# Loads cut into other pieces, a planner with other landing times, and raw products in the last two column pieces of a fused FFT-filter and GeGLU kernel

## The chip, the cores and the metric

The kernel runs on one core of one Trainium2 chip. The metric is the device time of one execution in microseconds (us). The core's engines are named as the profile names them: PE (matrix multiply, with its weight loads as PEld), DVE (vector), ACT (activation functions and copies), POOL (GpSimd) and SP, which here does nothing but issue DMAs.

## The reference

One input x (2048 x 640, bf16) is layer-normalised row by row into xn. Two branches start from xn and meet at the end:

```
xn = layernorm(x)
s  = irfft2(rfft2(xn) * (w_r + 1j * w_i))              # a filter in the frequency plane
g  = silu((gelu(xn @ w_gate) * (xn @ w_up)) @ w_down)  # 640 -> 1536 -> 640
out = x + s * g
```

## The kernel before, in words

**Tiles.** The 2048 rows are sixteen slabs of 128 rows (n1 = 0 to 15), kept in `X`. The hidden size 1536 is cut into twelve tiles of 128 (t), the slabs into four groups of four (grp).

**The GeGLU branch.** `gate_up(grp, t)` (L878) makes two psum tiles: five matmuls of 512 columns into `pg` (gate) and five into `pu` (up), all at L891. ACT turns `pg` into `ge` with Gelu (L904), DVE multiplies `pu` by `ge` into `uT` (L908). There are two buffers each of `pg` and `pu` and three of `ge`, so the gate matmuls of tile t+2 wait for the Gelu of tile t, and the up matmuls of t+2 for the product of t. `down(n1)` (L935) then makes one slab's 640 output columns from twelve `uT` tiles and `Wd` (L969), in two pieces of 320 columns, 2 x 6 matmuls each; the last slab (n1 = 15) has three pieces of 256, 256 and 128 columns. A piece goes through a tanh on ACT (L978) and a product on DVE (L983), which together are SiLU; `finish` (L951, L956) multiplies by the filter branch y and adds x.

**The start.** The first four slabs are transposed on PE while they are still raw (`turn_raw`, L461) and copied into `XR` (L297; helper `copy_on`, as are all copies out of psum). The first two hidden tiles of group 0 run on these raw rows (L891 with `XR`); their results wait in `IU` and `R` and are normalised later on DVE (L921, L923) with the rows' means and deviations. For this those 2 x 4 x 128 numbers are turned on PE (L570), copied (L572, tile `th`), stored to DRAM (`D5`) and loaded back as a broadcast to all partitions (`RB`, 512 KB). Column sums of the first weights come from one-column matmuls (L472). From slab 4 on, normalised slabs are transposed by DMA (L502).

**The filter branch.** `fold` adds and subtracts mirrored halves on DVE (L511 to L525), a DFT of 128 points follows on PE (L538, L539), ACT copies the result into `mc` (two buffers), and a DMA stores it to DRAM (`D2`, one store for each pair of slabs, eight in all). When all eight are stored, DRAM is read back regrouped (`BU`, L583), and `spectral` (L659 to L778) and `inverse` (L812 to L836) do the rest of the transform.

**The order.** Nothing in the program's order is left to the hardware. Every piece of work is a `Task` with an engine, a cost, a rank and its predecessors; `Plan.run` plays them through with the costs written in the code, always taking the ready task of best rank, and the engines' instruction streams are emitted in the order that it finds. `Plan.ready` gives the time from which a task may start: the latest of its predecessors' ends plus `MARGIN` (250 ns for PE, 60 ns for the others). A DMA's end is `land` where one is given; otherwise it is the modelled end on the wire (340 bytes per ns) plus a term that depends on when it was issued. So a changed cost does not change what an engine does, but when the plan lets it do it: the order on all engines may change.

**The loads.** All loads of the start but one are issued by SP, in the order in which the code adds them: 0.4 to 1 us of SP for one, so that the order on SP is the order on the wire. A DMA that SP issues also waits until the DMA eight places before it on the hardware queues has landed, since completions go round eight semaphores.

Of the kernel before, what the change touches and what calls it, by code (L numbers as in the profile page):

```python
# [13 lines left out]
ACT = mybir.ActivationFunctionType  # L14
ALU = mybir.AluOpType
P = 128
S = 2048
D = 640
# [96 lines left out]
class Plan:  # L115
# [21 lines left out]
    def ready(self, t, e, now):  # L137
        for a in t.after:
            if a.done is None:
                return None  # L140
        for a in t.order:
            if a.start is None:
                return None
        at = max([0.0] + [a.start + a.engs[e][0] if a.on == e == "PE" else a.done + (0 if a.on == e and not a.size else self.MARGIN[e] + ((1500 if a.size else 250) if e == "PE" and a.start > 20000 else 0)) for a in t.after])
        more = {}
        for s in t.new:
            mine = self.slots[s.tag]
            k = len(mine) - self.bufs[s.tag] + more.get(s.tag, 0)
            more[s.tag] = more.get(s.tag, 0) + 1
            if k >= 0:  # L150
                for u in mine[k].users:
                    if u.done is None:
                        return None
                    at = max(at, u.done + self.MARGIN[e])
        if t.size and e == "SP":
            at = max(at, self.wire - self.BACKLOG)
        return at

    def run(self):
        left, now, order = list(self.tasks), 0.0, []  # L160
        while left:
            best, soon, held = None, None, {}
            for t in left:
                if t.hold:
                    for e in t.engs:
                        at = self.ready(t, e, now)
                        if at is not None and now < at <= now + t.hold:
                            held[e] = min(held.get(e, t.rank), t.rank)
            for t in left:
                for e in t.engs:  # L170
                    at = self.ready(t, e, now)
                    if at is None:
                        continue
                    at = max(at, self.free[e])
                    if at <= now and e in held and held[e] < t.rank:
                        at = now + 20
                    if at <= now and len(t.engs) > 1 and e == "DVE" and max(now, self.free["ACT"]) + t.engs["ACT"][0] <= now + t.engs[e][0] + self.PREFER:
                        at = max(now, self.free["ACT"]) + 20
                    if at <= now:
                        if best is None or (t.rank, t.seq) < (best[0].rank, best[0].seq):  # L180
                            best = (t, e)
                    elif soon is None or at < soon:
                        soon = at
            if best is None:
                if soon is None:
                    raise AssertionError("the plan is stuck at %d of %d" % (len(order), len(self.tasks)))
                now = soon
                continue
            t, e = best
            occ, lat = t.engs[e]  # L190
            t.on, t.start = e, now
            self.free[e] = now + occ
            if VERB: print(f"{now:9.0f} {occ:6.0f} {t.done or 0:9.0f} {e} {t.emit.__qualname__.split('kernel.<locals>.')[-1]} {t.rank}")
            t.done = now + lat
            if t.land:
                self.wire = max(self.wire, t.land - 3200)
                t.done = t.land
            elif t.size:
                self.wire = max(self.wire, now + occ + 900) + t.size * t.slow / 340.0
                t.done = self.wire + (1000 if now < 1000 else 2100 if now < 1700 else 2600 if now < 2700 else 3300 if now < 18000 else 2600 if now < 21000 else 1000) + t.lag  # L200
            for s in t.new:
                self.slots[s.tag].append(s)
            order.append(t)
            left.remove(t)
        return order
# [17 lines left out]
def kernel(  # L223
# [11 lines left out]
    nc = tc.nc  # L235
# [95 lines left out]
    def load_w(sb, view, got, a, b, land=0):  # L331
        cs = slice(a * P, b * P)
        seq[0] += 1
        w = dma(sb[:, :, cs], view[:, :, cs], (0, -4, seq[0]), (b - a) * 163840, slow=1.1, land=land)
        for t in range(a, b):
            got[t] = w
# [33 lines left out]
                                 start=True, stop=True, skip_group_check=True)  # L370
        return add(go, "PE", (n * ns, n * ns), rank, after=after, new=[] if heat.users else [heat], use=[idle] + ([heat] if heat.users else []))
    seq[0] += 1
    x_in[0] = add(lambda e: None, "SP", (1, 1), (0, -5), size=1, land=3550)
    load_w(Wg, gv, g_in, 0, 2, land=4500)
    load_x(1, 2, land=4950)
    load_w(Wu, uv, u_in, 0, 2, land=6150)
    load_x(2, 3, land=6600)
    load_x(3, 4, land=7100)
    t = add(blank, "DVE", (330, 400), (0, -9), new=[idle])
    t = warmed = keep_warm(6, [t])  # L380
    load_gu(2, 4)
# [1 line left out]
    load_tab("f1")  # L383
    load_x(6, 8)
    load_gu(4, 6)
    load_x(8, 10)
    load_gu(6, 8)
    load_x(10, 12)
    load_gu(8, 10)
    load_x(12, 16)  # L390
    load_gu(10, 12)
    load_d(0, 8)
    load_d(8, 12)


    aps, roots = {}, {}
# [538 lines left out]
    def down(n1):  # L935
# [26 lines left out]
        for lo, hi, tag in parts:  # L962
            ps, th, mm = Slot(tag), Slot("th"), []
            for k in range(0, 12, 6):
                def go(e, k=k, lo=lo, hi=hi, ps=ps):
                    if k == 0:
                        place(ps, (512,))
                    for i in range(k, k + 6):
                        nc.tensor.matmul(ps.tile[:, 0:hi - lo], lhsT=uT[grp, ks[i]].tile[:, j * P:(j + 1) * P], rhs=Wd[:, ks[i], lo:hi],  # L969
                                         start=(i == 0), stop=(i == 11))  # L970
                step[0] += 1
                mm.append(add(go, "PE", c_pe(*[hi - lo] * 6), (1, step[0]), new=[] if k else [ps],
                              after=[u_done[grp, t] for t in ks[k:k + 6]] + mm + [d_in[t] for t in ks[k:k + 6]],
                              use=[uT[grp, t] for t in ks[k:k + 6]] + ([ps] if k else [])))

            def tanh(e, lo=lo, hi=hi, ps=ps, th=th):
                place(th, (320,), FP32)
                nc.scalar.activation(out=th.tile[:, 0:hi - lo], in_=ps.tile[:, 0:hi - lo], func=ACT.Tanh, scale=0.5)  # L978

            def silu(e, lo=lo, hi=hi, ps=ps, th=th):  # L980
                if lo == 0:
                    place(G2, (D,))
                nc.vector.scalar_tensor_tensor(out=G2.tile[:, lo:hi], in0=th.tile[:, 0:hi - lo], scalar=1.0, in1=ps.tile[:, 0:hi - lo],  # L983
                                               op0=ALU.add, op1=ALU.mult)
            def early(e, lo=lo, hi=hi, ps=ps):
                place(yp, (hi - lo,), FP32)
                nc.vector.tensor_tensor(out=yp.tile, in0=y.tile[:, n1 % 2, lo:hi], in1=ps.tile[:, 0:hi - lo], op=ALU.mult)

            def late(e, lo=lo, hi=hi, th=th):
                nc.vector.scalar_tensor_tensor(out=yg.tile[:, lo:hi], in0=th.tile[:, 0:hi - lo], scalar=1.0, in1=yp.tile,  # L990
                                               op0=ALU.add, op1=ALU.mult)
            a = add(tanh, "ACT", c_act(hi - lo), (0, step[0]), after=mm[-1:], new=[th], use=[ps])
            if last and hi == D:
                yp = Slot("mc")
                t = add(early, "DVE", c_dve(hi - lo, 1, True), (0, step[0]), after=mm[-1:] + [y_done[n1]], new=[yp], use=[ps, y])
                t = add(late, "DVE", c_dve(hi - lo, 1), (0, step[0]), after=[a, t] + done, use=[th, yp, yg])
                t = add(lambda e, lo=lo: nc.vector.tensor_tensor(out=res.tile[:, lo:], in0=yg.tile[:, lo:], in1=sx.tile[:, lo:], op=ALU.add),
                        "DVE", c_dve(hi - lo), (0, step[0]), after=[t, xr], use=[yg, sx, res])
                add(lambda e, lo=lo: nc.scalar.dma_start(out=outv[:, n1, lo:], in_=res.tile[:, lo:]), "ACT", (430, 430), (0, 0, n1),
                    after=[t], use=[res], size=256 * (hi - lo))  # L1000
                continue
            done.append(add(silu, "DVE", c_dve(hi - lo, 1, True), (0, step[0]), after=[a] + done, new=[] if lo else [G2],
                            use=[ps, th, G2] if lo else [ps, th]))
            if last:
                finish(lo, hi, [done[-1]], (0, step[0]), lo == 0)
# [42 lines left out]
```

## Time and profile before

| | |
|---|---|
| median of 4 runs | 204.67 us (204.38 to 204.81) |
| the profiled execution's own time | 204.43 us |
| its span in the trace | 202.7 us, so 1.7 us lie around it |
| granted TensorE clock | 0.999 |
| PE busy | 196.0 us, 97% of the span |
| DVE, ACT, POOL busy | 146.8, 127.3, 33.7 us |
| DMA in the first 30 us | 320 to 395 GB/s from slice 2 to slice 6 of 40, mean 161 GB/s over the span |
| last matmul ends, last store issued, span ends | 198.3, 200.06, 202.7 us |

A matmul of N columns counts as busy longer than it holds the engine, because matmuls overlap: five of 512 columns appear as a row of 1.24 us but the next group starts 1.08 us after them (0.216 us each). A stall on PE is therefore read from the distance of starts, not only from the idle column. Six matmuls of 320 columns take 0.81 us in this sense, twelve 1.63 us, and one 128-column matmul at the start 0.056 us.

### The profile page before, as it was taken

The page shows a single profiled execution, that of the slowest core. Times are in us where ns is not written, and L with a number is a line of the kernel's source. Part 1 is how long each engine was busy: PE and PEld are TensorE (multiplying, and loading weights), DVE is VectorE, ACT ScalarE, POOL GpSimd, SP SyncE. Part 2 cuts the span into 40 slices and gives each one's busy share as a digit, 9 for nine tenths or more (in the row PEclk, how much of TensorE's full clock was granted, in tenths as well). Part 3 has the DMA queues.
Part 4 walks back from the last instruction along what each step waited for, and adds up shares of the span by engine and source line. Part 5 has one row for each costly group of instructions (what it writes and reads, how often), then busy time and mean ns, then how long its engine had stood idle before and what let it go on. Part 6 is the DMA issues. An engine that isn't in the chain of part 4 may idle for free.

```text
span 202.7 us, 4151 instructions
## 1 busy us (share of the span) xinstructions
PE 196.0 (97%) x1547; PEld 117.8 (58%) x1547; DVE 146.8 (72%) x314; ACT 127.3 (63%) x228; POOL 33.7 (17%) x72
## 2 busy tenths in 40 slices
PE   7999999999999999999999999999999999999991
PEld 2994443567544554677755554567755555557781
DVE  3689849999522227999999989963326987778782
ACT  4998759984543466687776757433276666765521
POOL 2413134599400000000000000000000222112212
PEclk9999999999999999999999999999999999999999
DMA  6999999568883958664430411014900333344422
GB/s 174 325 320 338 335 395 218 127 84 203 215 287 113 375 161 243 115 144 138 128 114 24 129 65 65 3 65 129 418 38 0 108 83 108 102 127 129 132 100 65
DMA packets 35398, 32.62 MB, mean 161 GB/s; under 512 B 10798, under 2 KB 32306, under 8 KB 35378
## 3 DMA queue, kind: packets, MB, share of 16 engines
q1 hardware_dynamic: 33938, 29.49, 49.0%
q0 software_dynamic: 1152, 2.66, 5.7%
q10 hardware_dynamic: 288, 0.20, 0.6%
q8 instruction: 12, 0.20, 0.4%
q14 instruction: 8, 0.07, 0.1%
HBM read 22.51 MB, written 9.19 MB: 156 GB/s over the span
## 4 chain that ended last, share of the span: by engine, by line
PE 79%; DMA 10%; DVE 6%; SPq 2%; issue 1%; ACT 1%; DVEq 0%; ACTq 0%
PE pg L891 20%; PE pu L891 20%; PE pg L969 11%; PE pu L969 11%; DMA RB<-D 4%; DMA D<-th 3%; PE sp L703 3%; PE sp L836 3%; PE sp L778 2%; PE sp L812 2%; DMA X<-in_A_x_dram 2%; PE sp L676 2%; SPq L502 1%; DMA D<-in_A_w_r_dram 1%; PE sp L696 1%
## 5 line engine op out<-in xcount | busy, mean ns | idle before, releaser
L891 PE MATMUL pg<-xnT,Wg 128*128 128x512 bf16 (+1 forms) x245 | 57.3, 366 | 0.3 <-ACT ge L904 0.3
L891 PE MATMUL pu<-xnT,Wu 128*128 128x512 bf16 (+1 forms) x245 | 57.3, 366 | 0.0
L908 DVE TENSOR_TENSOR uT<-pu,ge 128x512 bf16<-128x512 f32 x46 | 31.7, 688 | 27.5 <-PE pu L891 25.2
L904 ACT ACTIVATE ge<-pg 128x512 bf16<-128x512 f32 x46 | 27.3, 596 | 30.6 <-PE pg L891 30.5
L969 PEld LDWEIGHTS <-uT 128*128 128x128 bf16 x396 | 37.7, 98 | 14.3 <-issue 0.4
L891 PEld LDWEIGHTS <-Wg 128*128 128x128 bf16 x285 | 25.2, 98 | 23.9 <-issue 0.6
L891 PEld LDWEIGHTS <-Wu 128*128 128x128 bf16 x285 | 24.8, 98 | 20.7 <-issue 0.3
L932 POOL DMA_DIRECT2D xr<-in_A_x_dram x16 | 8.8, 550 | 133.0 <-DVE res L956 133.0
L969 PE MATMUL pg<-Wd,uT 128*128 128x320 bf16 (+2 forms) x204 | 30.5, 293 | 0.0
L969 PE MATMUL pu<-Wd,uT 128*128 128x320 bf16 (+1 forms) x192 | 29.5, 297 | 0.1
L297 ACT CAST ma<-sp 128x644 bf16<-128x644 f32 (+1 forms) x32 | 23.4, 794 | 7.4 <-PE sp L703 3.4
L297 ACT CAST IU<-sp 128x640 bf16<-128x640 f32 x16 | 10.7, 693 | 3.9 <-PE sp L778 3.9
L297 ACT CAST Vt<-sp 128x640 bf16<-128x640 f32 x16 | 10.8, 691 | 3.7 <-PE sp L812 3.7
L978 ACT ACTIVATE th<-pg 128x320 f32<-128x320 f32 (+2 forms) x17 | 7.2, 426 | 9.3 <-PE pg L969 8.6
L297 ACT CAST mc<-sp 128x640 bf16<-128x640 f32 x16 | 10.6, 699 | 4.0 <-DMA D<-mc 3.9
L983 DVE SCALAR_TENSOR_TENSOR G<-th,pg 128x320 bf16<-128x320 f32 (+1 forms) x16 | 7.7, 478 | 6.2 <-ACT th L978 6.1
L978 ACT ACTIVATE th<-pu 128x320 f32<-128x320 f32 (+1 forms) x16 | 7.0, 439 | 8.0 <-PE pu L969 7.9
L983 DVE SCALAR_TENSOR_TENSOR G<-th,pu 128x320 bf16<-128x320 f32 (+1 forms) x16 | 7.7, 479 | 5.6 <-ACT th L978 5.5
L431 POOL TENSOR_TENSOR RSTD<-MVA,mh 128x1 f32<-128x1 f32 x12 | 8.9, 746 | 2.9 <-DVE MVA L413 2.2
L416 ACT ACTIVATE th<-X 128x640 bf16<-128x640 bf16 x11 | 8.1, 737 | 0.5 <-DMA D<-th 0.4
L756 DVE TENSOR_TENSOR R<-Y 64x644 bf16<-64x644 bf16 x16 | 7.8, 490 | 0.4
L758 DVE TENSOR_TENSOR R<-Y 64x644 bf16<-64x644 bf16 x16 | 7.8, 486 | 0.3
(110 smaller groups left out, 240.1 us busy)
## 6 DMA issues: line engine op xcount, KB each, us to landing
BU<-D SPq DMA_DIRECT2D x8, 640.0 KB
D<-mc SPq DMA_DIRECT2D x8, 320.0 KB
xr<-in_A_x_dram POOLq DMA_DIRECT2D x16, 160.0 KB, 3.5
D<-IU SPq DMA_DIRECT2D x8, 320.0 KB
out_dram<-res SPq DMA_DIRECT2D x15, 160.0 KB
Wg<-in_B_w_gate_dram SPq DMA_DIRECT2D x6, 320.0 KB
Wu<-in_B_w_up_dram SPq DMA_DIRECT2D x6, 320.0 KB
WF<-D SPq DMA_DIRECT2D x8, 161.0 KB
```

The lines of the kernel that those rows point to most:

```text
L297: return nc.scalar.copy(out=out, in_=in_) if e == "ACT" else nc.vector.tensor_copy(out=out, in_=in_)
L416: nc.scalar.activation(out=place(junk, (D,)), in_=x, func=ACT.Copy, scale=-1.0 / D, accum_out=less)
L431: nc.gpsimd.tensor_tensor(out=rstd, in0=var, in1=mh, op=ALU.pow)
L756: nc.vector.tensor_tensor(out=o, in0=Yf[:, ::-3, :], in1=Yf[:, 1:3, :], op=ALU.subtract)
L758: nc.vector.tensor_tensor(out=o, in0=Y[:, 0], in1=Y[:, 1], op=ALU.add)
L891: nc.tensor.matmul(ps.tile[:, lo:hi], lhsT=w[:, c, t * P:(t + 1) * P], rhs=XR[:, c, lo:hi] if early else xnT[:, c, grp * 512 + lo:grp * 51 ...
L904: nc.scalar.activation(out=ge.tile, in_=pg.tile if src is None else src, func=ACT.Gelu_apprx_tanh)
L908: nc.vector.tensor_tensor(out=u.tile, in0=pu.tile if src is None else src, in1=ge.tile, op=ALU.mult)
L932: nc.gpsimd.dma_start(out=sx.tile, in_=xv[:, n1, :])
L969: nc.tensor.matmul(ps.tile[:, 0:hi - lo], lhsT=uT[grp, ks[i]].tile[:, j * P:(j + 1) * P], rhs=Wd[:, ks[i], lo:hi], start=(i == 0), stop=(i ...
L978: nc.scalar.activation(out=th.tile[:, 0:hi - lo], in_=ps.tile[:, 0:hi - lo], func=ACT.Tanh, scale=0.5)
L983: nc.vector.scalar_tensor_tensor(out=G2.tile[:, lo:hi], in0=th.tile[:, 0:hi - lo], scalar=1.0, in1=ps.tile[:, 0:hi - lo], op0=ALU.add, op1 ...
```

## The change

Four edits. The matmuls, the copies and their shapes stay the same in number (1547 matmuls in both); on PE, DVE, ACT and POOL the order of instructions moves, SP issues six loads of late x slabs where it issued three, and six loads of Wd where it issued two.

The planner:

```diff
-        at = max([0.0] + [a.start + a.engs[e][0] if a.on == e == "PE" else a.done + (0 if a.on == e and not a.size else self.MARGIN[e] + ((1500 if a.size else 250) if e == "PE" and a.start > 20000 else 0)) for a in t.after])
+        at = max([0.0] + [a.start + a.engs[e][0] if a.on == e == "PE" else a.done + (0 if a.on == e and not a.size else (self.MARGIN[e] if a.start > 9000 else 60) + ((1500 if a.size else 250) if e == "PE" and a.start > 20000 else 0)) for a in t.after])
...
-                t.done = self.wire + (1000 if now < 1000 else 2100 if now < 1700 else 2600 if now < 2700 else 3300 if now < 18000 else 2600 if now < 21000 else 1000) + t.lag
+                t.done = self.wire + (1000 if now < 1000 else 2100 if now < 1700 else 2600 if now < 2700 else 3300 if now < 18000 else 2600 if now < 27000 else 1000) + t.lag
```

The landing times given for the first loads, and the pieces of the later ones:

```diff
-    x_in[0] = add(lambda e: None, "SP", (1, 1), (0, -5), size=1, land=3550)
-    load_w(Wg, gv, g_in, 0, 2, land=4500)
-    load_x(1, 2, land=4950)
-    load_w(Wu, uv, u_in, 0, 2, land=6150)
-    load_x(2, 3, land=6600)
-    load_x(3, 4, land=7100)
+    x_in[0] = add(lambda e: None, "SP", (1, 1), (0, -5), size=1, land=3620)
+    load_w(Wg, gv, g_in, 0, 2, land=4690)
+    load_x(1, 2, land=5200)
+    load_w(Wu, uv, u_in, 0, 2, land=6790)
+    load_x(2, 3, land=7280)
+    load_x(3, 4, land=7750)
...
     load_gu(4, 6)
-    load_x(8, 10)
+    load_x(8, 9)
+    load_x(9, 10)
     load_gu(6, 8)
-    load_x(10, 12)
+    load_x(10, 11)
+    load_x(11, 12)
     load_gu(8, 10)
-    load_x(12, 16)
+    load_x(12, 14)
+    load_x(14, 16)
     load_gu(10, 12)
-    load_d(0, 8)
-    load_d(8, 12)
+    for a in range(0, 12, 2):
+        load_d(a, a + 2)
```

The last slab: the form that only the last piece had (`early`: y times the raw psum; `late`: tanh plus one, times that product; then the add of x) is now that of the second piece, too, each with its own buffer `yp`, and the second piece is stored by SP:

```diff
+            yp = Slot("mc")
...
-            if last and hi == D:
-                yp = Slot("mc")
+            if last and lo:
                 t = add(early, "DVE", c_dve(hi - lo, 1, True), (0, step[0]), after=mm[-1:] + [y_done[n1]], new=[yp], use=[ps, y])
                 t = add(late, "DVE", c_dve(hi - lo, 1), (0, step[0]), after=[a, t] + done, use=[th, yp, yg])
-                t = add(lambda e, lo=lo: nc.vector.tensor_tensor(out=res.tile[:, lo:], in0=yg.tile[:, lo:], in1=sx.tile[:, lo:], op=ALU.add),
+                t = add(lambda e, lo=lo, hi=hi: nc.vector.tensor_tensor(out=res.tile[:, lo:hi], in0=yg.tile[:, lo:hi], in1=sx.tile[:, lo:hi], op=ALU.add),
                         "DVE", c_dve(hi - lo), (0, step[0]), after=[t, xr], use=[yg, sx, res])
-                add(lambda e, lo=lo: nc.scalar.dma_start(out=outv[:, n1, lo:], in_=res.tile[:, lo:]), "ACT", (430, 430), (0, 0, n1),
-                    after=[t], use=[res], size=256 * (hi - lo))
+                if hi == D:
+                    add(lambda e, lo=lo: nc.scalar.dma_start(out=outv[:, n1, lo:], in_=res.tile[:, lo:]), "ACT", (430, 430), (0, 0, n1),
+                        after=[t], use=[res], size=256 * (hi - lo))
+                else:
+                    dma(lambda lo=lo, hi=hi: outv[:, n1, lo:hi], lambda lo=lo, hi=hi: res.tile[:, lo:hi], (0, 0, n1), 256 * (hi - lo), after=[t], use=[res])
                 continue
```

What the built orders show: at the start PE does the column sums of Wg in two halves around the transposes of slab 1, and starts the gate matmuls of slab 1 before the up matmuls of slab 0; all four copies of transposed slabs (`xnT`) go to ACT, where DVE had two. On SP the store `D5` stands before the last X load, the first `D2` store behind 640 KB of Wd instead of 1280 KB, and `RB` behind 960 KB instead of 1280 KB. The regrouped filter branch starts about 2 us of PE work earlier against the GeGLU branch. At the end of DVE the order is: product of piece 1, `early` and `late` of piece 2, `early` of piece 3, add of piece 2, `late` and add of piece 3; on SP piece 2 is stored ahead of piece 1.

More of the change, by code (lines that the diff above doesn't have):

```diff
@@ L984, in silu, with early, late @@
                                                op0=ALU.add, op1=ALU.mult)
-            def early(e, lo=lo, hi=hi, ps=ps):
+            yp = Slot("mc")
+            def early(e, lo=lo, hi=hi, ps=ps, yp=yp):
                 place(yp, (hi - lo,), FP32)
                 nc.vector.tensor_tensor(out=yp.tile, in0=y.tile[:, n1 % 2, lo:hi], in1=ps.tile[:, 0:hi - lo], op=ALU.mult)
-            def late(e, lo=lo, hi=hi, th=th):
+            def late(e, lo=lo, hi=hi, th=th, yp=yp):
                 nc.vector.scalar_tensor_tensor(out=yg.tile[:, lo:hi], in0=th.tile[:, 0:hi - lo], scalar=1.0, in1=yp.tile,
```

## The prediction

> **What bounds the kernel now.** I read the page first, then the timeline of PE, then those of ACT and DVE where PE stalls.
>
> ```profile
> PE 196.0 (97%) x1547; PEld 117.8 (58%) x1547; DVE 146.8 (72%) x314; ACT 127.3 (63%) x228; POOL 33.7 (17%) x72
> ```
>
> PE is busy for 97% of the span, at a granted clock of 0.999, and the change adds and removes no matmul. So the time is PE's work plus PE's stalls plus the two ends. The timeline has PE back to back from 5.33 us to 198.3 us, except in one stretch:
>
> ```profile
> 30.28 1.24 PE L891 MATMUL pu<-xnT,Wu 128*128 128x512 bf16 x5
> 31.82 1.24 PE L891 MATMUL pg<-xnT,Wg 128*128 128x512 bf16 x5 [0.30 <-ACT ge L904]
> 33.06 1.24 PE L891 MATMUL pu<-xnT,Wu 128*128 128x512 bf16 x5
> 34.14 1.24 PE L891 MATMUL pg<-xnT,Wg 128*128 128x512 bf16 x5
> ...
> 36.33 0.97 PE L969 MATMUL pg<-Wd,uT 128*128 128x320 bf16 x6
> 37.39 0.97 PE L969 MATMUL pu<-Wd,uT 128*128 128x320 bf16 x6
> 38.20 1.98 PE L969 MATMUL pg<-Wd,uT 128*128 128x320 bf16 x12
> 40.02 0.98 PE L969 MATMUL pu<-Wd,uT 128*128 128x320 bf16 x6
> ...
> 42.19 1.79 PE L969 MATMUL pu<-Wd,uT 128*128 128x320 bf16 x12
> 44.22 0.38 PE L538 MATMUL sp<-mb,F1T 128*128 128x512 bf16 x1 [0.24 <-ACT mc L297]
> ```
>
> Read the starts, against 1.08 us for five 512-column matmuls, 0.81 for six of 320 and 1.63 for twelve. 30.28 to 31.82 is 0.46 too long, 31.82 to 33.06 is 0.16, 36.33 to 37.39 is 0.25, 38.20 to 40.02 is 0.19, 42.19 to 44.22 is 0.40: together **1.46 us**, all that can be won between the ends. Who is late? In the timeline of ACT, and in the waits of 24 to 46 us:
>
> ```profile
> 26.55 0.58 ACT L904 ACTIVATE ge<-pg 128x512 bf16<-128x512 f32 x1
> 29.18 0.69 ACT L297 CAST mc<-sp 128x640 bf16<-128x640 f32 x1 [2.05 <-DMA D<-mc]
> ...
> 31.16 0.61 ACT L904 ACTIVATE ge<-pg 128x512 bf16<-128x512 f32 x1
> ```
>
> ```profile
> DVE IU L921 <- DMA RB<-D: 2.2, 1, 2.2
> ACT mc L297 <- DMA D<-mc: 2.1, 1, 2.1
> ```
>
> ACT stands 2.05 us before a copy into `mc`, whose buffer the first D2 store still reads (landed 29.18). Behind it in ACT's order is the Gelu of tile 8 (31.16), for which PE waits at 31.82. DVE stands 2.17 us for the broadcast RB (landed 30.39). From there both engines work without a break (31.36 to 36.33: 4.97 of 4.97 us each), and the later stalls of PE are this backlog.
>
> **The change, part by part.** The terms are differences to the profiled execution (204.43 us; span 202.7).
>
> *Wd in six loads.* The first D2 store now follows 640 KB of Wd, not 1280. In 10 to 32 us the DMAs move 337 GB/s on average, without a pause, so 640 KB less ahead is 1.9 us: the store lands at about 27.2. RB has 320 KB less ahead: 1.0 us, about 29.4. In the new order ACT reaches this copy later (about 28.0, below), so its wait goes altogether. That is the larger part of the gain: I follow the new order with the old durations. ACT: Gelu of tile 7 at 27.5 (0.5 from start to start), copy 28.0, a statistic 28.6, copy 29.3, Gelu of tile 8 at 29.9 to 30.5. PE wants it at about 31.7: no stall. The next are the Gelu of tile 9, ready about 32.5, wanted 33.9, and tile 10, 34.4 for 36.0. DVE: RB 29.4, two L921 (0.67 each), but it first has the product of tile 7, so the product of tile 8 ends near 31.7, wanted 32.8; tile 9 33.5 for 34.9; tile 10 36.05 for 36.8; tile 11 38.25 for 38.4. The last is too close for comfort, and the fold behind it (39.2) may wait 0.15. I take **-1.25 of the 1.46**, with the ends -0.5 (the backlog stays) and -1.46.
>
> Against the split speaks the Trainium skill, "DMA: Bandwidth & Descriptors", section "Bandwidth": batch transfers to at least 1 MiB for three quarters of the peak rate. By it the six loads of 320 KB would be slower than the one of 1280 KB. The rows here speak for the trace: while SP issues loads of 160 to 320 KB, from 10 to 18 us, the DMAs already run at the rate that they keep later, since up to eight are under way at once; I count no loss.
>
> *Late x slabs in smaller loads.* Three more issues on SP. SP spends about 1.0 us on 320 KB here (18.68, 17.63), so it is paced by the wire, and an issue alone costs 0.4 (17.19): hidden. D5 passes one 320 KB load: 15.8 instead of 16.80, landing about 22.0 instead of 22.97 (6.17 us as in the row). Nothing on PE waits for these slabs before 50 us; without this cover an issue costs 0.4 each, 1.2 at most, which only moves D5 and RB back to their old places.
>
> *Planner with later first landings.* It moves the first 15 us. Now:
>
> ```profile
> 5.31 0.74 ACT L416 ACTIVATE th<-X 128x640 bf16<-128x640 bf16 x1 [0.15 <-DMA X<-in_A_x_dram]
> 5.95 0.19 ACT L416 ACTIVATION_READ_ACCUMULATOR th<-X 128x1 f32 x1
> 6.04 0.67 ACT L297 COPY XR<-sp 128x640 bf16<-128x640 bf16 x1
> ```
>
> The copy of raw slab 1 is ready at 6.71. Before, PE filled the time with up matmuls of slab 0 (6.43) and used slab 1 at 7.53. In the new order: half of the Wg sums before slab 1's transposes, in the gap that PE has anyway (5 x 0.028, a gain of 0.14 if Wg has landed by 5.2); transposes 5.34, sums 5.62, two gate groups 5.76 to 6.32 (5 x 0.056 each), and then at once the gate group of slab 1, which needs the copy: PE waits from 6.32 to about 6.77, 0.45. The rest I followed to 15 us: everything is ready when PE comes, though ACT has two copies more (2 x 0.69) and DVE two less. Sum **+0.3**; ends -0.14 (DVE or ACT gets to the copy sooner) and +0.6 (also the Wg half waits).
>
> *Wait in the other new places.* The statistic of slab 6 on ACT takes the `th` buffer that D5 still reads; behind it stands the Gelu of tile 5. With D5 at 22.0 this Gelu ends at 23.2, and PE wants it at 24.7: hidden, 0.
>
> *After 44 us.* PE has no stall there now. In the new order the first matmuls on BU (L676) stand two groups of 1.08 us earlier. BU was issued at 62.82, and used at 69.1: 6.3 us. With 4.1 it should still land (640 KB at the 375 GB/s of that slice are 1.75 us, and the `xr` row shows 3.5 us to landing for 160 KB). Take **0**, ends 0 and +0.8.
>
> *Raw products in the last pieces.* The tail now:
>
> ```profile
> 198.09 0.42 DVE L983 SCALAR_TENSOR_TENSOR G<-th,pu 128x256 bf16<-128x256 f32 x1 [0.49 <-ACT th L978]
> 198.21 0.67 POOL L956 TENSOR_TENSOR res<-yg,xr 128x256 bf16<-128x256 bf16 x1
> 198.34 0.28 ACT L978 ACTIVATE th<-pg 128x128 f32<-128x128 f32 x1 [0.28 <-PE pg L969]
> 198.65 0.29 DVE L987 TENSOR_TENSOR mc<-s,pg 128x128 f32<-128x128 bf16 x1
> ```
>
> The `early` product that exists already (L987) starts at 198.65, not when PE ends but when the tanh of the same psum tile ends (198.34 + 0.28). So it does not run beside the tanh, and that of piece 2 will not either. What is left is the order: G, and six operations 0.20 apart, end at 199.67. After: `early` and `late` of 256 columns, about 0.34 each (G's 0.42 less the overlap), 198.09 to 198.77; then 0.20 four times, 0.21 for the last: 199.6. The last store may now be that of piece 1 behind piece 2 on SP, at the same time. **-0.05**; ends -0.15 and +0.2.
>
> The Trainium skill, "PSUM — Partial Sum Buffer", section "PSUM bank collisions raise a hardware error", speaks against this edit in the same sense: two engines must not read one bank at a time, so software has to order them. By it the raw product is late by a tanh, as the row at 198.65 shows; if the two did run together, the tail would gain about 0.4.
>
> *Sum:* -1.25 + 0.3 + 0 + 0 - 0.05 = -1.0, so 203.4 for an execution like the profiled one. That one lay 0.24 below the median of 204.67; against the median I say **203.7 us**.
>
> **Rivals.**
> *The backlog stays* (about the same time). ACT is the full engine from 31 to 42 us, and it gets 1.4 us more copies at the start. If the later stalls stay (0.25 + 0.19 + 0.40) and only the first two go: -0.62 + 0.3 = -0.3, 204.4. For it: 4.97 of 4.97 us busy. Against it: the 2.05 us that ACT no longer stands still.
>
> *ACT waits for D5* (slower). ACT stands with the statistic of slab 6 until D5 lands, and the Gelu of tile 5 is behind it. It decides from a landing at 23.4 on (0.72 for the statistic, 0.5 for the Gelu, wanted at 24.7). If the 4 KB need 9 us instead of 6.17, landing at 24.8, PE waits 1.4 us, and the backlog stays: +1.4 + 0.3 - 0.3 = +1.4, 206.1. Against it: D5 has fewer bytes ahead.
>
> *BU is late* (about the same). The filter branch wants BU 2.2 us earlier; if it lands at the old distance of 6 us, PE waits up to 1.9 us at L676, less 1.0 won: +0.9, 205.6; half of it gives 204.6.
>
> **How the numbers follow.** Forecast 0.6 (203.2 to 204.2), backlog stays 0.17, ACT waits for D5 0.08, BU late 0.15. A measurement of this kernel tells about 0.2%, 0.4 us, from no change. Faster by more: the forecast and a bit of the first rival, 0.63. Same: the rest of the first rival, half of BU, 0.2. Slower: 0.17. The best sum (-1.46 - 0.14 - 0.15) gives 202.9, hardly likely to hold in all terms; 8 in 10 is 203.1 to 205.0.
>
> **What would show it.** After: no wait of ACT on `D<-mc` near 28 us, DVE's wait on RB ending about 29.4; starts of PE from 28 to 45 us 1.08, 0.81, 1.63 apart; one gap of about 0.45 near 6.4 us; first L676 with no idle before it; the product of piece 2 starting when its tanh ends, the last add ending 1.3 us after the last matmul. A wait of PE on ACT near 24.7 us or on BU would make the prediction wrong.

## The result, and the profile after

The changed kernel took 205.65 us (median of 34 runs, 204.56 to 208.22) where the kernel before took 204.72 (52 runs). The ratio is 1.0043, with a 95% interval of 1.0032 to 1.0055: slower by 0.43%, about 0.9 us, where the forecast was 203.7 us and faster. The first execution of it that was profiled (207.84 us) was a disturbed one with a granted clock of 0.985, so the profile shown here as "after" is that of a later one, from experiment e10: 205.52 us, which is the median of its series (205.51), at a clock of 1.000. Its lines stand 3 above those of before (L891 is now L894, L969 is L972).

The line of the page on busy time. 17 of the 1547 matmul records are missing in this trace (the weight loads are complete), so PE's sum is not to be compared to the tenth:

```profile
span 203.7 us, 4147 instructions
PE 195.3 (96%) x1530; PEld 118.2 (58%) x1547; DVE 147.4 (72%) x312; ACT 129.6 (64%) x230; POOL 33.6 (16%) x72
```

The timeline of PE in the stretch in which before had all its stalls:

```profile
30.65 1.24 PE L894 MATMUL pu<-xnT,Wu 128*128 128x512 bf16 x5
31.73 1.24 PE L894 MATMUL pg<-xnT,Wg 128*128 128x512 bf16 x5
32.80 1.24 PE L894 MATMUL pu<-xnT,Wu 128*128 128x512 bf16 x5
...
36.04 0.98 PE L972 MATMUL pg<-Wd,uT 128*128 128x320 bf16 x6
36.86 0.98 PE L972 MATMUL pu<-Wd,uT 128*128 128x320 bf16 x6
37.67 0.98 PE L972 MATMUL pg<-Wd,uT 128*128 128x320 bf16 x6
38.49 0.98 PE L972 MATMUL pu<-Wd,uT 128*128 128x320 bf16 x6
39.30 0.38 PE L541 MATMUL sp<-mb,F1T 128*128 128x512 bf16 x1
```

The starts are 1.08 and 0.81 us apart: nothing is left of the 1.46 us of stalls. The timelines of ACT and of DVE show why:

```profile
27.61 0.69 ACT L297 CAST mc<-sp 128x640 bf16<-128x640 f32 x1 [0.51 <-PE pu L894]
...
29.50 0.61 ACT L907 ACTIVATE ge<-pg 128x512 bf16<-128x512 f32 x1
```

```profile
29.64 0.75 DVE L924 SCALAR_TENSOR_TENSOR IU<-RB,WSUM,IU 128x512 f32<-128x512 f32 x1 [0.46 <-DMA RB<-D]
```

ACT's copy into `mc` no longer waits for a store, the Gelu of tile 8 starts at 29.50 instead of 31.16, and DVE's wait for `RB` is 0.46 us instead of 2.17. So the part of the change that the forecast lived on worked. The time was lost in a place where before had no stall at all. The view of PE's waits in the whole execution after has these three (total, times, longest); the first, at the start, is in before, too, and only a gap of 0.26 us at 6.8 us, told below, is not among them:

```profile
PE sp L369 <- DVE uT L362: 1.2, 1, 1.2
PE sp L781 <- DVE R L759: 1.2, 1, 1.2
PE sp L781 <- DVE R L761: 0.3, 1, 0.3
```

The timeline of PE around them:

```profile
89.56 0.98 PE L972 MATMUL pu<-Wd,uT 128*128 128x320 bf16 x6
91.73 0.47 PE L781 MATMUL sp<-R,TI 128*128 128x256 bf16 x4 [1.20 <-DVE R L759]
92.04 0.98 PE L972 MATMUL pu<-Wd,uT 128*128 128x320 bf16 x6
93.28 0.48 PE L781 MATMUL sp<-R,TI 128*128 128x256 bf16 x4 [0.26 <-DVE R L761]
```

From start to start, 2.17 us stand where 0.81 are needed, and then 1.24 for 0.81: 1.36 + 0.43 = 1.79 us of PE are lost. L781 is the first matmul of the filter's way back for the third of eight groups of columns; it needs `R`, which DVE makes. DVE, then:

```profile
85.56 0.82 DVE L746 TENSOR_TENSOR mc<-WF,mb 128x1288 bf16<-128x1288 bf16 x1
89.14 0.83 DVE L738 TENSOR_TENSOR mc<-WF,mb 128x1288 bf16<-128x1288 bf16 x1 [2.77 <-DMA WF<-D]
89.89 0.49 DVE L749 TENSOR_TENSOR Y<-mc 128x644 bf16<-128x644 bf16 x1
...
91.19 0.49 DVE L759 TENSOR_TENSOR R<-Y 64x644 bf16<-64x644 bf16 x1
```

DVE stands 2.77 us before a product with `WF`, the filter weights of that group, and behind it are the two operations that PE wants. The load that it waits for (`WF<-D`, L632: the weights read back in reversed order from a scratch copy in DRAM) is issued by SP, and the timeline of SP says when, in after and then in before:

```profile
83.83 0.60 SPq L609 DMA_DIRECT2D D<-in_A_w_r_dram  x1
84.47 0.60 SPq L609 DMA_DIRECT2D D<-in_A_w_i_dram  x1
85.11 0.63 SPq L632 DMA_DIRECT2D WF<-D  x1
```

```profile
86.04 0.60 SPq L606 DMA_DIRECT2D D<-in_A_w_i_dram  x1
86.68 0.63 SPq L629 DMA_DIRECT2D WF<-D  x1
```

And the same product on DVE in before:

```profile
90.79 0.82 DVE L735 TENSOR_TENSOR mc<-WF,mb 128x1288 bf16<-128x1288 bf16 x1
```

This is the whole case in three numbers each. The load takes 4.03 us from its issue on SP to the start of the product that waits for it (85.11 to 89.14; 3.7 to 4.1 in the runs below). In before it was issued at 86.68 and used at 90.79, 4.11 us later, without a wait: the weights came just in time, with 0.4 us to spare at most, and a list of waits does not show that. In after DVE is ready at 86.37, 4.4 us sooner; SP issues the load at 85.11, only 1.6 us sooner, because SP works through a chain of its own: the regrouped read `BU`, for whose landings two loads behind it wait 1.8 and 2.1 us, then twelve copies of weights into the scratch `D4`, mostly 0.60 us each (L609). The new order and the missing stalls moved PE, ACT and DVE ahead of a queue that did not move with them.

### The profile page after: what moved, and what is told of

The parts are those of the page before. It is cut to its first block, busy times and chain, and to the rows that moved or that the text cites. A ratio compares the mean times of both kernels' runs of the same rounds, so it can differ in the third digit from the quotient of the medians.

```text
span 206.0 us, 4164 instructions
## 1 busy us (share of the span) xinstructions
PE 198.0 (96%) x1547; PEld 118.9 (58%) x1547; DVE 147.4 (72%) x312; ACT 129.5 (63%) x230; POOL 33.7 (16%) x72
## 4 chain that ended last, share of the span: by engine, by line
PE 80%; DMA 9%; SPq 4%; DVE 3%; ACT 1%; issue 1%; DVEq 0%
PE pg L894 21%; PE pu L894 21%; PE pg L972 11%; PE pu L972 11%; DMA BU<-D 5%; SPq L609 3%; PE sp L839 3%; DMA WF<-in_A_w_r_dram 2%; PE sp L815 2%; PE sp L781 2%; DMA WF<-D 2%; PE sp L541 2%; PE sp L369 1%; PE sp L706 1%; PE sp L833 1%
## 5 line engine op out<-in xcount | busy, mean ns | idle before, releaser
L894 PE MATMUL pg<-xnT,Wg 128*128 128x512 bf16 (+1 forms) x245 | 57.4, 366 | 0.0
L894 PE MATMUL pu<-xnT,Wu 128*128 128x512 bf16 (+1 forms) x245 | 57.3, 366 | 0.0
L972 PEld LDWEIGHTS <-uT 128*128 128x128 bf16 x396 | 38.3, 99 | 14.2 <-issue 0.2
L894 PEld LDWEIGHTS <-Wg 128*128 128x128 bf16 x285 | 25.1, 98 | 22.4 <-issue 0.2
L894 PEld LDWEIGHTS <-Wu 128*128 128x128 bf16 x285 | 25.0, 98 | 21.8
L972 PE MATMUL pg<-Wd,uT 128*128 128x320 bf16 (+2 forms) x204 | 31.9, 300 | 0.0
L972 PE MATMUL pu<-Wd,uT 128*128 128x320 bf16 (+1 forms) x192 | 29.5, 297 | 0.0
L986 DVE SCALAR_TENSOR_TENSOR G<-th,pu 128x320 bf16<-128x320 f32 x15 | 7.3, 485 | 5.3 <-ACT th L981 5.1
L781 PE MATMUL sp<-R,TI 128*128 128x256 bf16 (+1 forms) x64 | 7.4, 239 | 1.9 <-DVE R L759 1.7
L738 DVE TENSOR_TENSOR mc<-WF,mb 128x1288 bf16<-128x1288 bf16 x8 | 6.6, 825 | 3.4 <-DMA WF<-D 3.2
L857 DVE TENSOR_TENSOR mb<-ma 128x640 bf16<-128x640 bf16 x8 | 3.9, 492 | 7.0 <-ACT ma L297 7.0
```

What stands on the lines that cost most here:

```text
L738: nc.vector.tensor_tensor(out=sM.tile, in0=sw.tile, in1=sV.tile, op=ALU.mult)
L781: nc.tensor.matmul(pt[:, pq, at:at + 2 * (hi - lo)], lhsT=TI[:, 2 * G + h, :], rhs=v[:, :, lo:hi], start=True, stop=True, skip_group_check ...
L894: nc.tensor.matmul(ps.tile[:, lo:hi], lhsT=w[:, c, t * P:(t + 1) * P], rhs=XR[:, c, lo:hi] if early else xnT[:, c, grp * 512 + lo:grp * 51 ...
```

## Experiments

The theory after this reading: the forecast gain is real, the filter weights of the third group take it back, and the new tail costs a bit more. The rivals: the smaller loads cost wire time, the clock or `BU` explains the time, or the tail alone does. A wait is given with the instruction that has it.

**e0, the changed kernel again.** No edit.

> The changed kernel once more, for its profile beside the others. Theory (filter weights late): PE stands about 1.9 us and 0.4 us before the two L781 groups near 90 us, because DVE's product L738 of the third filter group waits 2 to 3 us for the load WF<-D; the time is 204.6 to 207, varying with the landing of that load. Rival (the clock alone): the granted clock dips somewhere in every execution that is slow, whether PE stands still before it or not.

205.4 us (9 runs, 204.71 to 209.63), ratio 1.0036 (1.0012 to 1.006). In its profiled execution, which is its fastest (204.71), the load is issued at 84.64, DVE waits 1.88 us, and PE loses 0.48 + 0.42, less than the 1.9 + 0.4 expected.

**e1, the weights earlier.** In the changed kernel the load `WF<-D` of the third group is put behind six of the twelve `D4` copies instead of all twelve (it needs only the two of its own group, which come first):

```diff
-        for t in plan.run():
+        order = plan.run()
+        order.remove(W_in[2])
+        order.insert(order.index(turned_w[4][1]) + 1, W_in[2])
+        for t in order:
```

> The changed kernel with one SP instruction moved: the load of the third filter group's reversed weights (WF<-D, L632) is issued behind the sixth of the twelve loads into D4 instead of behind the last; all other engines keep their order. Theory (filter weights late): issued near 81.5 us instead of 85.7, landed near 85.5, so DVE no longer waits and PE no longer stands before L781: 1.9 + 0.4 us and the slow clock after it go, 203.5 us against 204.7 for the kernel before (ratio 0.994), with the clock at 1.0. Rival (smaller loads cost): still 205.6. Rival (the clock alone): still 205 to 206, with a dip of the clock.

203.98 us (203.61 to 204.12), ratio 0.9955 (0.9943 to 0.9967). The load on SP and the product on DVE in e1:

```profile
80.88 0.63 SPq L632 DMA_DIRECT2D WF<-D  x1
```

```profile
86.36 0.82 DVE L738 TENSOR_TENSOR mc<-WF,mb 128x1288 bf16<-128x1288 bf16 x1
```

The load is issued at 80.88, the product starts at 86.36 without a wait, and the view of PE's waits has only the one at the start. One line on SP, moved by 4 us, turns the change from a loss to a gain: the theory's main point holds.

**e2, Wd in six loads alone**, in the kernel before:

```diff
-    load_d(0, 8)
-    load_d(8, 12)
+    for a in range(0, 12, 2):
+        load_d(a, a + 2)
```

> The kernel before with the one part that loads Wd in six pieces. In its built order the filter branch stands where it stood before. Theory: the first D2 store lands 1.9 us earlier, RB 1.0 us earlier, the stalls of PE between 31 and 44 us shrink from 1.46 to 0.5 or less, and nothing is late at 90 us: 203.7 (ratio 0.995). Rival (smaller loads cost): slower than before by 0.3 us or more.

204.21 us, ratio 0.9972 (0.996 to 0.9985): a gain, but less than the 203.7 us expected. The rival that the smaller loads cost time falls. ACT's wait on `D<-mc` goes from 2.1 to 0.8 us, the first two stalls of PE go (0.62 us), the later three stay (0.14 + 0.18 + 0.41), and the weights are waited for here, too (issued at 87.89, product at 91.92 after 1.29 us, PE 0.42).

**e3, the planner and its landing times alone**, in the kernel before (both planner lines and the six `land` values of the diff).

> The kernel before with the planner's part alone (landing times and margins). In its built order the filter branch stands 2.2 us of PE work earlier, as in the changed kernel. Theory (filter weights late): PE stands before the third filter group's inverse matmuls near 90 us, 1 to 2.5 us, and the stalls of 31 to 44 us remain in part: 205 to 207, slower than before. Rival (smaller loads cost): no smaller loads here, so 204.7 or less.

204.29 us, ratio 0.9978 (0.9964 to 0.9993). The expectation missed. With Wd still in two loads, the new order alone clears all stalls from 31 to 44 us: it lets ACT and DVE do other work until `RB` and the store have landed, so that ACT waits for no DMA in 10 to 46 us and DVE for none but one x slab (0.6 us). PE loses 0.39 us to the weights (issued 84.27, product at 88.01).

The next four ran on another chip.

**e4, e1 with the tail of before.** The diff of the last slab is undone:

```diff
-            if last and lo:
+            if last and hi == D:
+                yp = Slot("mc")
```

> The changed kernel with the filter weights of the third group loaded earlier (as in e1) and with the tail of before (raw product in the last piece only). Theory: the new tail costs 0.35 us (last matmul group to last store issue 2.59 us in e0 and e1; 2.24 to 2.3 with the old tail), so this one gains that on e1: about 203.6 us, ratio 0.993 to 0.9945, and the distance from the last group of twelve matmuls on PE to the last store issue is 2.2 to 2.3 us. Rival, the prediction's step: the new tail is worth 0.05 us, so undoing it changes nothing or costs 0.05: 204.0 us, ratio 0.9955 to 0.996, distance 2.6.

203.02 us (202.78 to 203.32), ratio 0.9914 (0.9898 to 0.9929), the fastest kernel of the case. The distance from the last twelve matmuls to the last store issue is 196.44 to 198.68 = 2.24 us, as the theory had it; the time gained on e1 is more than that (see the tail below).

**e5, the new tail alone**, in the kernel before.

> The kernel before with the new tail alone (raw products in the last two pieces). Theory: +0.3 to +0.4 us against before, ratio 1.0015 to 1.002, and the second piece's `late` of 256 columns takes 0.6 us on DVE where the prediction had 0.34. Rival, the prediction's step: -0.05 us, ratio 0.9995 to 1.0.

204.82 us, ratio 1.0001 (0.9991 to 1.0011). The rival, the prediction's step, is nearer here than the theory, though the distance from the last twelve matmuls to the last store issue does grow a little, from 2.24 to 2.38 us, and `late` takes 0.42 us, not 0.6. The profile tells why: the order on DVE is another one. These are the tail on DVE and on POOL, first in e5:

```profile
198.53 0.29 DVE L989 TENSOR_TENSOR mc<-s,pg 128x128 f32<-128x128 bf16 x1
198.74 0.62 DVE L992 SCALAR_TENSOR_TENSOR yg<-th,mc 128x256 bf16<-128x256 f32 x2
```

```profile
198.09 0.67 POOL L956 TENSOR_TENSOR res<-yg,xr 128x256 bf16<-128x256 bf16 x1
```

and then in after (e10):

```profile
198.77 0.42 DVE L992 TENSOR_TENSOR mc<-s,pu 128x256 f32<-128x256 bf16 x1 [0.70 <-ACT th L981]
199.22 0.62 DVE L995 SCALAR_TENSOR_TENSOR yg<-th,mc 128x256 bf16<-128x256 f32 x1
199.77 0.28 DVE L992 TENSOR_TENSOR mc<-s,pg 128x128 f32<-128x128 bf16 x1
```

```profile
198.90 0.67 POOL L959 TENSOR_TENSOR res<-yg,xr 128x256 bf16<-128x256 bf16 x1
```

In e5 the `early` of the last piece (198.53) stands ahead of the `late` of piece 2, and the row at 198.74 holds both `late` operations, 256 and 128 columns: 0.62 us for the two, of which the first has 0.42 (0.34 from start to start). In after `late` of piece 2 has 0.62 us alone. The shape, the operands and the types are the same; what differs is that in e5 POOL's add of piece 1 has ended (198.09 + 0.67 = 198.76) and in after it runs until 199.57. `late` ends at 199.84, 0.27 after it.

**e6, the weights later.** In the changed kernel the same load goes behind two further weight loads.

```diff
-        for t in plan.run():
+        order = plan.run()
+        order.remove(W_in[2])
+        order.insert(order.index(W_in[3].order[0]) + 1, W_in[2])
+        for t in order:
```

> The changed kernel with the same weights loaded still later on SP, behind two further weight loads, some 1.3 us. Theory: the stall on PE at the inverse matmuls of the third group follows the load one for one, 0.8 us in the undisturbed run of the changed kernel, so some 2.1 us here and 206.0 to 206.6 us, more (up to 207.5) if PE runs at a lower clock after the longer pause; ratio 1.006 to 1.012; the wait of DVE's cast on this load grows from 1.9 to about 3.2 us. Rival, the time of the changed kernel comes from something else in the filter branch (the regrouping, the order) and the load is only near it: 205.5 us, ratio 1.003 to 1.005.

207.06 us (205.96 to 208.78, 4 runs), ratio 1.0113 (1.0058 to 1.0167). The load is issued at 87.25 and the product starts at 91.19 after 2.85 us, in the expected size. PE, however, loses at L781 only 1.43 + 0.43 us, since it comes there late: it had waited 1.60 us for `BU`. The timeline of PE in e6:

```profile
67.78 1.07 PE L679 MATMUL sp<-T,BU 128*128 128x128 bf16 x16 [1.60 <-DMA BU<-D]
```

The edit can't have caused that, as it moves a load that SP issues 20 us later. In e6 `BU` was issued at 62.88, in e0 at 60.98 with the first L679 at 65.9, and no wait. PE's loss for the weights (1.86 us) is that of e10 (1.79); what this profile loses beyond e10 is the wait for `BU`. So e6 shows neither the price of later weights nor that they are slower, and the proof rests on e1 and its repeat, e8. That `BU` is late, the prediction's rival, does happen in some executions.

**e7, the x slabs in smaller loads alone**, in the kernel before (the six `load_x` of the diff for the three).

> The kernel before with the late x slabs in smaller loads alone; Wd in two loads, old planner times, old tail. The filter branch of its built order starts 2.2 us earlier on PE, as in the changed kernel. Theory: the stalls of the first 31 to 44 us stay at least in part (the Wd loads are still ahead of the first store), the weights of the third group are waited for by 1 to 2 us on DVE, and PE loses 0.3 to 0.8 us near 90 us: 204.7 to 205.6 us, ratio 1.0 to 1.004. Rival: smaller x loads already let the store and the statistics' broadcast land early enough, as the planner edits alone did: 204.2 us, ratio 0.997 to 0.998.

204.89 us (204.64 to 207.32), ratio 1.0025 (0.9998 to 1.0053): not to be told from no change. The profiled execution is its slowest (207.32): there SP holds for 3.75 us at the issue of `RB`, which lands at 31.04, and PE waits 1.9 us for the product of tile 8. The wait for the weights that was expected isn't there (issued at 86.47, product at 90.48). With Wd in two loads the smaller x loads help nothing, and the rival falls.

**e8 to e11**, on one chip, to have the tail and the weights side by side. e8 is e1 again, e9 is e4 again, e10 the changed kernel, and e11 is e8 with the raw products in bf16 (they are rounded once more):

```diff
-                place(yp, (hi - lo,), FP32)
+                place(yp, (hi - lo,))
```

> e1 again, now on one chip with the next three, so that the tail can be told apart from the chip. Theory: 203.6 to 204.1 us, 0.4 to 0.6 us above the version with the old tail, since the last twelve matmuls to the last store issue take 2.59 us with the new tail and 2.24 with the old one. Rival, the tail is worth nothing either way (alone it made 1.0001 of the kernel before): both versions give the same time, and the 0.96 us between e1 and e4 was the chip.

> e4 again, beside e8: weights of the third group earlier, old tail. Theory: 202.8 to 203.4 us, ratio 0.990 to 0.994, 0.4 to 0.6 us below e8. Rival, the tail is worth nothing: as e8, within 0.2 us.

> The changed kernel once more, for another profile of it and for its spread beside e8 and e9 on one chip. Theory: 205.0 to 205.8 us, over 1.3 us above e8, and the profile has PE waiting before the inverse matmuls of the third group for 0.7 to 2 us, with DVE's cast on the weights' load. If the regrouped read BU is late in this execution, its wait stands before the filter's first matmuls on it and the weights' wait is shorter by about as much. Rival, the spread of the changed kernel (204.56 to 208.22) comes from BU alone: the profile shows BU's wait and none on the weights.

> e8 with the raw products of the last two pieces kept in bf16 instead of float32 (the products are rounded once more). Asked: why `late` of 256 columns takes 0.62 us where the prediction had 0.34. Theory: it reads the float32 product, so with bf16 it takes 0.35 to 0.45 us, and the time is 0.1 to 0.3 us below e8. Rival: it shares something with the add of piece 1 that POOL runs at the same moment (198.12 to 198.79), and takes 0.55 to 0.62 us here too.

| on one chip | median us | ratio to before | 95% interval |
|---|---|---|---|
| before | 204.71 | 1 | |
| e10: the changed kernel | 205.51 | 1.0040 | 1.0020 to 1.0059 |
| e8: weights earlier | 203.89 | 0.9959 | 0.9946 to 0.9972 |
| e11: e8, products in bf16 | 203.87 | 0.9956 | 0.9943 to 0.9968 |
| e9: weights earlier, old tail | 203.07 | 0.9927 | 0.9907 to 0.9946 |

By the medians the change is made of three parts: -1.64 us that the loads and the planner bring when the weights are in time (e9 to before), +0.82 that the tail costs (e8 to e9; +0.66 by the ratios, whose intervals just touch at 0.9946), and +1.62 that the weights' wait costs (e10 to e8; PE's loss in e10's profile is 1.79). They add up to the +0.80 between e10 and before.

e11 answers that the float32 product, the theory there, is not what makes `late` slow: with bf16 it is 0.62 us as before, and the time is that of e8. In e0, e1, e8, e10 and e11 `late` of 256 columns begins 0.32 to 0.33 us after the start of POOL's add, takes 0.62, and ends 0.27 to 0.28 us after POOL's add has ended. The Trainium skill, "SBUF — State Buffer", section "SBUF: two separate sides", states that VectorE and GpSimd share a pair of ports under an exclusive lock, that an operation of VectorE with two inputs in SBUF needs it against a GpSimd operation that reads SBUF, and that the later of the two is blocked until the other has ended. These rows agree: `late` reads `th` and `mc`, both in SBUF, while `early` beside the same add, with one input in psum, takes 0.42 us in e0 and e5 alike. The other way round, POOL's product of piece 1 (L951 in before) takes 0.85 us in before and e5, where it starts while DVE adds two SBUF tiles (L956), and 0.66 to 0.67 in e0, e1, e8, e9 and e10, where no such operation runs beside it. A run in which POOL's add alone is moved away wasn't made, so the cause rests on these rows.

## Why the prediction was wrong

**The stalls from 31 to 44 us: right.** The prediction took -1.25 of 1.46; all of it went in e10, e0, e1 and e8. DVE uses `RB` at 29.64 (forecast 29.4), ACT's copy starts at 27.61 (28.0), the Gelu of tile 8 ends at 30.1 (30.5). The spot that it called too close, the product of tile 11 and the fold behind it, is indeed the narrow one: in the first profiled execution and in e6, e9 and e11 0.2 to 0.4 us of stalls came back at 38 to 40 us. What it did not see is that two parts of the change reach this by themselves: the planner alone clears all five stalls (e3), Wd alone the first two (e2). The rival "the backlog stays" is what e2 shows.

**The start, +0.3: right in place, its size not settled.** PE has a gap of 0.26 us at 6.8 us in e10, the wait that was forecast (0.45). The size can be read in e4, where PE loses nothing else. The last group of matmuls, first in before and then in e4:

```profile
197.47 0.83 PE L969 MATMUL pg<-Wd,uT 128*128 128x128 bf16 x12
```

```profile
196.44 0.83 PE L972 MATMUL pg<-Wd,uT 128*128 128x128 bf16 x12
```

It comes 1.03 us sooner, though 1.46 us of stalls are gone, so some 0.4 us went at the start, near the forecast. But the profiled execution of before was quick there: its first gate group starts at 5.88, and those of e5, e7 and e2, whose order at the start is the same, at 5.96, 5.98 and 6.19. So part of +0.3 was counted against a lucky row, and the price against the median stays open. The medians do not give it either: e9 gains 1.64 us, more than the stalls, but its end is shorter, too: from the start of that group to the end of the span e4 and e9 take 4.76 us and before takes 5.19, with the same tail; why is open.

**The other waits, 0: right, with a wrong step.** `D5` was to be issued at 15.8 instead of 16.80; in e10 it is issued at 17.14. It lands soon enough all the same: ACT waits 0.3 us for it at the statistic (L419), 1.7 and 1.8 in e6 and e11, and PE has no wait near 24.7 us in any of them. Smaller x loads have no measurable price (e7).

**After 44 us, 0: this step failed.** The prediction said "PE has no stall there now" and then followed one transfer, `BU`, to its first matmuls. It did see that the filter branch comes 2.2 us earlier and that a transfer might not follow; it asked this of the first transfer of the branch only. The branch is fed by a second one, the weights, that hangs on SP's own chain, and there was hardly any slack: issue to use was 4.11 us in before, against the 3.7 to 4.1 that it takes. Both rows were in the trace of before (SP at 86.68, DVE at 90.79). That SP would issue the load 1.6 us earlier and DVE be ready 4.4 us earlier, which makes the wait of 2.8 us, only the runs could tell; but the prediction's own 2.2 us of earlier use, against at most 0.4 to spare, asked for a term here, or for a reason why SP would come earlier by as much. On PE the wait costs less: in e0, e2, e3 and e10 PE loses 0.9 to 1.0 us less than DVE waits (0.90 for 1.88, 0.42 for 1.29, 0.39 for 1.35, 1.79 for 2.77). That `BU` would just land in time was right in e0 and e10 and wrong by 1.6 us in e6, and where it was right there was luck in it: PE comes to it at 65.83 in e10, 3.3 us sooner than in before and not 2.2, and it is in time because `BU` is issued at 60.84 instead of 62.82, which the prediction did not count.

**The tail, -0.05: wrong, and the wrong sign.** The mechanism that was named held: `early` of piece 2 starts at 197.99 in e0, when its tanh ends (197.57 + 0.39), not when PE ends. What failed is the term "`early` and `late` of 256 columns, about 0.34 each": in e0 `late` takes 0.62, 0.54 from start to start, and `early` 0.46 from start to start. Together they take 0.32 more than forecast; the last add ends 1.7 us after the last matmul, not 1.3, and the last store issue moves from 2.24 to 2.59 us behind the start of the last matmul group. The forecast took `late` as if it ran alone, when the row of POOL's add at the same time stood in the very fence that was shown. A second part, about 0.3 us, lies between the last store's issue and the end of the span (2.82 in e8, 2.53 in e9). From the start of the last matmul group to the end of the span it makes 5.4 us in e1, e8 and e11 against 4.76 in e4 and e9, so 0.66 in all, which is the price by the ratios. The second part would go with three stores issued within 0.5 us at the end in place of two, as piece 1 now stands behind piece 2 on SP; but before itself shows 2.99 there with the old tail, so that part stays open. In the order of before the same tail costs next to nothing (e5: 5.32 us to the end of the span, before 5.19), so the price goes with the new order on the engines, not with the edit alone. (The prediction counts six operations behind G where the trace has five, and its 199.6 fits four behind `late`, not five; that changes nothing here.)

**The range** ended at 205.0 since the only slow cases in it were `D5` and `BU`. In the sum, the forecast of -1.0 is -1.64 + 0.82 + 1.62 = +0.80.

## What to carry to other kernels

When a change makes one part of a kernel run ahead, list every transfer that the later parts wait for, on each queue, and write beside each the time from its issue to its first use: one that is used as soon as it lands shows no wait today and may show one tomorrow. A queue that is paced by its own transfers does not come earlier because the engines do, so the gain is given back at the first load that had no slack; here one load moved by half a dozen places on SP was worth 1.6 us of 205. And before an operation is priced by another row, look what the neighbouring engine does in the same microsecond.

## What the runs showed of the hardware

- PE's speed at the start differs between executions of the same order: the two 512-column matmuls near 4.3 us take 0.59 us in before and 1.06 in e2, whose start is the same, and the first gate group starts at 5.88 and 6.19. The profiled execution of before had the quick one.
- In the first profiled execution of the changed kernel PE paused 1.69 us for the weights, until 92.41. From 94 to 96 us the granted clock was 0.54 and from 96 to 98 us 0.61, and two groups of six 320-column matmuls took 1.80 and 1.37 us instead of 0.98. After pauses of 1.20 us (e10), 1.60 (e6, for `BU`) and 1.91 (e7) the granted clock stayed at 1.00. So the length of the pause alone did not decide; what did is not known.
